# Preparing the first attention job one pair earlier, weight splits one by one, and loads in program order

## The chip, the cores and the metric

The kernel runs on one core of a Trainium2 chip. Its time is device microseconds, from runs on the chip: 737.43 us as a median of three runs (737.38 to 737.55). Every other time below is from one profiled execution of the kernel before, which took 735.49 us; its span, from the first recorded instruction to the last, is 733.8 us.

## The reference

Three stages follow each other; everything is float32.

```python
# attention: 2 batches, 8 heads, 576 rows, head size 64, causal, with a bias from cumulated s
scores = scale * q @ k.T;  cum = cumsum(max(s, 0))
scores = where(causal, -1e9, scores + min(-(cum_i - cum_j), 0))
x = softmax(scores) @ v                      # -> 1152 tokens x 512
# experts: all 4 for every token, weighted by p
out = sum over e of p[:, e] * (relu(x @ w1[e]) @ w2[e])      # 512 -> 1024 -> 512
# gated layer
y = ((out @ wa) * (out @ wb)) @ wo                           # 512 -> 1536 -> 512
```

## The kernel before

**How products are made.** Most products are made of three matmuls each: both operands are split into a high part that TensorE takes in its float32r format and a low part, the rest (`mm3`, line 276: high by high, high by low, low by high). A split is one copy on ACT (ScalarE) for the high part and one subtraction on VectorE (DVE) or GpSimd (POOL) for the low one. Weights are split this way too, in pieces of 512 KB: `load_next` (line 240) issues the load of a piece into one of three `raw` buffers, `split_next` (244) splits the oldest loaded one, `weight_step` (250) does one load and one split.

**The head.** Rows 0 to 255 of the first batch, for all eight heads, are done first, from `qk0` and `v0` (loop at line 896). Two heads make a pair; `pair_out` (line 832) divides the pair's result on VectorE (838), turns it on TensorE and copies it on ACT to `x32` (846) and to `xh` (847). There are four pairs.

**The attention.** What is left of the attention is cut into groups of row tiles, three of them, each with eight jobs, one per head. A job is loaded by `load_job` (569: `qr`, `kr`, and `kb` rows of the cumulated bias), prepared by `prep_job` (580: high part `qh` on ACT, low part `qb` on VectorE, high part `ks` on ACT, whose upper half goes by DMA into `kb` (589), and the low half of `ks` on GpSimd (590)), and then goes through one step per row tile: scores (616, 617), row maxima (627), exponential (639), division (644 to 646), transposes (657), their copies `eh` and `el` (672, 673), and the product with `v` (689). `attn_step` (919) issues one step; a step issues work of five tiles in different states, and at a job's first tile it prepares the job after it and loads the one after that. The scores need both halves of `ks` and, for the second matmul, `kb`.

**What runs beside it.** While the attention runs, TensorE does the first tokens' experts: a plain float32 expert (`mm1`, line 1023, on `x32` and `w32`), then expert 1 in split form. Behind the attention come the other experts and the gated layer, in units of their own with weight loads and splits at a pace of 3 us of a modelled clock.

**What sets the order.** The program is put in order by a scheduler that keeps each engine's own order as a list. Three things restrict it around the change. `tc.issue_after(i)` keeps the instructions of its block behind instruction `i` in that list; `gated` (234) does it for the instructions in `gate`, here the fourth pair's lines 838 and 846, and for the first three attention steps and the first two splits (`gated(n < 3)`, `gated(nsplits[0] < 3)`). `queued` (549) keeps loads in program order as long as `early[0]` is true, which ends with the third step or at the first call of `attn_step` that finds it false. And a modelled clock paces the weight steps: `run` (1272) calls `weight_step` once for every 4 us of it beside the attention.

Of the kernel before, what the change touches and what calls it, by code (L numbers as in the profile page):

```python
# [12 lines left out]
AF = mybir.ActivationFunctionType  # L13
# [46 lines left out]
def fused_kernel(ctx, tc, qk0, v0, qT, kT, v, s, dp, w1, w2, wa, wb, wo, out):  # L60
    nc = tc.nc
# [137 lines left out]
    def split_piece(r, key, form, wide, src, j):  # L199
        wh, wl = slabs[key]  # L200
        if form == "half" and wide:
            t = pools["cv"].tile([P, SL], I32, tag="t", name="t")
            narrow(t, r[:, :, 0], r[:, :, 1])
            split(wh[:, j, :], wl[:, j, :], t.bitcast(F32), nc.gpsimd)
        elif form == "half":
            split(wh, wl, r, nc.gpsimd)
        elif form == "pair" and wide:
            if j == 0:
                wides[key] = pools["cv"].tile([P, NC, 2 * P], I32, tag="tp", name="tp")
            t = wides[key]  # L210
            narrow(t[:, 2 * j : 2 * j + 2], r[:, :, :, 0], r[:, :, :, 1])
            if j:
                split_pair(key, t.bitcast(F32), nc.gpsimd)
        elif form == "pair":
            split_pair(key, r, nc.vector)
        else:
            nsplit[0] += 1
            lo_eng = nc.gpsimd if nsplit[0] % 2 or nsplit[0] <= NFIRST else nc.vector
            two = slice(2 * j, 2 * j + 2)
            if nsplit[0] <= NFIRST:  # L220
                nc.gpsimd.tensor_scalar(
                    out=wh[:, two, :], in0=r, scalar1=1.0, scalar2=1.0, op0=ALU.mult, op1=ALU.mult
                )
            else:
                nc.scalar.activation(out=wh[:, two, :], in_=r, func=AF.Copy)
            for m in (2 * j, 2 * j + 1):
                lo_eng.tensor_tensor(
                    out=wl[:, m, :], in0=r[:, m - 2 * j, :], in1=wh[:, m, :].bitcast(F32), op=ALU.subtract
                )

    gate = []
    nsplits = [0]

    def gated(on):
        x = ExitStack()
        for i in gate if on else ():
            x.enter_context(tc.issue_after(i))
        return x

# [4 lines left out]
    def split_next():  # L244
        r, p_ = loaded.pop(0)
        nsplits[0] += 1
        with gated(nsplits[0] < 3):
            split_piece(r, *p_)

    def weight_step():  # L250
# [296 lines left out]
    early = [False]  # L547

    def queued(ins):
        return in_order(ins) if early[0] else ins  # L550
# [6 lines left out]
    x32 = [ckr[:, o : o + NT0] for o in (3 * S, 0, NT0, 2 * NT0)]  # L557
# [11 lines left out]
    def load_job(j):  # L569
        b, h = j.b, j.h  # L570
        j.qh = io_p.tile([P, j.nq], F32R, tag="qh", name=f"qh{j.nm}")
        j.qb = qbs[(j.h + 1) % 2]
        j.qr = rw_p.tile([P, j.nq], F32, tag="qr", name=f"qr{j.nm}")
        j.kr = rw_p.tile([P, j.nk], F32, tag="kr", name=f"kr{j.nm}")
        j.kb = io_p.tile([RB, j.nk], F32R, tag="kb", name=f"kb{j.nm}")
        queued(nc.sync.dma_start(out=j.qr, in_=qT[b, h, :, j.q0 : j.q1]))
        queued(nc.sync.dma_start(out=j.kr, in_=kT[b, h, :, : j.nk]))
        queued(nc.sync.dma_start(out=j.kb[D:, :].bitcast(F32), in_=ckD[:, PLACE[j.gi], h, : j.nk]))
# [41 lines left out]
    def st_softmax(j, i):  # L620
        t = j.t[i]
        t.e = e_p.tile([P, t.n], F32, tag="e", name=f"e{j.nm}_{i}")
        m0 = S - t.n
        seed = 3.0e38
        for ps, c0, c1 in t.ps:
            mn = st_p.tile([P, 1], F32, tag="mn", name="mn")
            nc.vector.tensor_tensor_reduce(
                out=t.e[:, c0:c1],
                in0=ps,
                in1=causal[:, m0 + c0 : m0 + c1],  # L630
                scale=-1.0,
                scalar=seed,
                op0=ALU.add,
                op1=ALU.min,
                accum_out=mn,
            )
            seed = mn
        t.l = st_p.tile([P, 1], F32, tag="l", name="l")
        nc.scalar.activation(out=t.e, in_=t.e, func=AF.Exp, bias=mn, scale=-1.0, accum_out=t.l)

    def st_norm(j, i):
        t = j.t[i]
# [104 lines left out]
    for base in (0, -32, -64, -96):  # L747
        nc.gpsimd.affine_select(
            out=sel_, in_=sel_, pattern=[[-1, H]], compare_op=ALU.not_equal,
# [5 lines left out]
        out=causal[:, S - P :], in_=causal[:, S - P :], pattern=[[-1, P]], compare_op=ALU.is_ge, fill=MASKED,  # L755
# [6 lines left out]
        out=cum[:NS, :NT0], data0=ones[:NS, :NT0], data1=sc[:, :NT0], initial=0.0,  # L762
# [3 lines left out]
        out=cb, in0=cum[:NS, :NT0], scalar1=1.0, scalar2=1.0, op0=ALU.mult, op1=ALU.mult  # L766
    ))
    for lo_, eng in ((slice(32, NB), nc.vector), (slice(96, NS), nc.gpsimd)):
        in_order(eng.tensor_tensor(
            out=cb[lo_], in0=cum[lo_, :NT0], in1=cb[lo_].bitcast(F32), op=ALU.subtract  # L770
# [56 lines left out]
        if h % 2:  # L827
            keep_warm(1)

    last = {}  # L830

    def pair_out(j):
        av = heads["av"]
        l, r = (st_p.tile([P, 2, 2], F32, tag=t, name=t) for t in "lr")
        nc.vector.tensor_scalar(out=l, in0=av[:, :, :, D], scalar1=1e-9, scalar2=None, op0=ALU.add)
        nc.vector.reciprocal(out=r, in_=l)
        xq = x_p.tile([P, 2, 2, D], F32, tag=("xs", "xt")[j % 2], name="xq")
        last["dve"] = nc.vector.tensor_tensor(
            out=xq, in0=av[:, :, :, :D], in1=r.unsqueeze(3).broadcast_to([P, 2, 2, D]), op=ALU.mult
        )  # L840
        ps = ps_a.tile([P, NT0], F32, tag="av", name="xT")
        for t in range(2):
            nc.tensor.transpose(
                ps[:, t * P : t * P + P], xq[:, t].rearrange("p a d -> p (a d)"), ident
            )
        last["act"] = nc.scalar.activation(out=x32[j], in_=ps, func=AF.Copy)
        nc.scalar.activation(out=xh[j][:, :NT0], in_=ps, func=AF.Copy)
        nc.gpsimd.tensor_tensor(
            out=xl[j][:, :NT0], in0=x32[j], in1=xh[j][:, :NT0].bitcast(F32), op=ALU.subtract
        )  # L850
# [36 lines left out]
    def shares():  # L887
        nc.gpsimd.tensor_tensor(out=den, in0=pr[:, :, 0], in1=pr[:, :, 1], op=ALU.add)
        for e in range(2, E):
            nc.gpsimd.tensor_tensor(out=den, in0=den, in1=pr[:, :, e], op=ALU.add)  # L890
        nc.vector.tensor_scalar(out=den, in0=den, scalar1=1e-9, scalar2=None, op0=ALU.add)
        nc.vector.reciprocal(out=den, in_=den)
        for e in range(E):
            nc.gpsimd.tensor_tensor(out=pr[:, :, e], in0=pr[:, :, e], in1=den, op=ALU.mult)
# [21 lines left out]
    def at(n):  # L916
        return seq[n] if 0 <= n < len(seq) else None

    def attn_step():
        n = state["n"]  # L920
        early[0] = early[0] and n < 3
        with gated(n < 3):
            attn_work(n)

    def attn_work(n):
        state["n"] += 1
        passed.append([])

        if x := at(n):
            j, i = x  # L930
            if i == j.i0:
                k = jobs.index(j)
                if k + 1 < len(jobs):
                    prep_job(jobs[k + 1])
                if k + 2 < len(jobs):
                    load_job(jobs[k + 2])
            st_enter(j, i)
        if x := at(n - 3):
            st_transpose(*x)
        if x := at(n):  # L940
            st_scores(*x)
        if x := at(n - 2):
            st_norm(*x)
        if x := at(n - 1):
            st_softmax(*x)
        if x := at(n - 4):
            j, i = x
            if i == j.i1 - 1:
                st_av(j)
        if x := at(n - 3):  # L950
            st_evac(*x)
        if x := at(n):
            j, i = x
            if i == j.i0:
                prep_v(j)
                k = jobs.index(j)
                if k + 1 < len(jobs):
                    load_v(jobs[k + 1])
# [250 lines left out]
    queued(nc.sync.dma_start(out=pr, in_=dp))  # L1209
    for _ in range(3):  # L1210
        load_next()
    with tc.issue_after(last["act"].ins), tc.issue_after(last["dve"].ins):
        prep_job(jobs[0])
        load_job(jobs[1])
        shares()
    gate.extend((last["act"].ins, last["dve"].ins))

    def keys_of(k):
        return () if k is None else k if isinstance(k[0], tuple) else (k,)
# [2 lines left out]
    after = pipelined(  # L1222
        [plain_stage(w, m, *TURNS[-1]) for w in halves[1] for m in range(NPR)]
        + [relu_stage(ex, m) for ex, m in lasts]
        + [None]
        + [ab_stage(m) for m in range(NTH * NPR)],
        True,
    )

    n = [k for k, u in enumerate(after) if u[0] == ("w1", halves[1][1])][-1]  # L1230
# [12 lines left out]
    for n in range(len(seq) + 12):  # L1243
        x = at(n)
# [10 lines left out]
        lead.append((u0, turn_t[g + 1] - SLACK, ends[g], ends[g + 1]))  # L1255

    PACE, LATE_PACE = 4.0, 3.0
    clock = {"t": 0.0, "w": 0.0}

    def advance(us):  # L1260

# [91 lines left out]
```

## Time and profile before

| | |
|---|---|
| median of three runs | 737.43 us |
| profiled execution / its span | 735.49 / 733.8 us |
| TensorE busy | 714.9 us, 97% |
| VectorE, GpSimd, ACT busy | 70%, 55%, 44% of the span |
| DMA | 61.42 MB, mean 84 GB/s |

A matmul in the profile is busy from its start to its modelled end, so TensorE's 97% says when it had work, not that it worked at its peak. Idle time of an engine is put down to what ended it: `[1.53 <-POOL ks L590]` means that the engine stood idle for 1.53 us before this instruction and that line 590 on GpSimd released it. PEld is TensorE's loading of weights, SPq the queue of DMA issues on SyncE, PEclk the granted clock of TensorE as a share of 2.4 GHz.

### The profile page before, as it was taken

The numbers are of one execution on the slowest core, as the hardware profiler recorded it, in microseconds if no ns is written. First come the engines' busy times: TensorE is split into PE (matmuls) and PEld (weight loads), VectorE is DVE, ScalarE is ACT, GpSimd is POOL, SyncE is SP. The second block draws the span as 40 slices with busy tenths as digits, with TensorE's granted clock in tenths as the row PEclk, the third lists the DMA queues.
The fourth block names the chain that finished last, engine by engine and source line by source line (L and its number), as shares of the span: only waits on it lengthen the run. The fifth ranks groups of instructions, "written<-read, shape, count | busy, mean of one in ns | idle before, by whom it ended". The sixth has DMA issues, their size and how long they took to land.

```text
span 733.8 us, 10985 instructions
## 1 busy us (share of the span) xinstructions
PE 714.9 (97%) x3878; PEld 622.7 (85%) x3880; DVE 514.6 (70%) x1055; ACT 325.9 (44%) x722; POOL 402.6 (55%) x333
## 2 busy tenths in 40 slices
PE   9889999999999999999999999999899999999998
PEld 5777789999899888888888888887798888878886
DVE  5467788767595876665655566599773979798674
ACT  3578799877633332330323133334455424252410
POOL 5567666756225634431333057686478878888500
PEclk9989999999999999999999999999999999999999
DMA  8574333433021202211111021222022222222003
GB/s 325 170 224 134 80 94 110 135 101 99 10 87 57 87 30 64 74 54 39 57 58 32 26 87 58 87 86 87 30 79 65 87 87 81 92 73 72 1 0 130
DMA packets 33580, 61.42 MB, mean 84 GB/s; under 512 B 3269, under 2 KB 17253, under 8 KB 33525
## 3 DMA queue, kind: packets, MB, share of 16 engines
q1 hardware_dynamic: 33045, 59.61, 25.9%
q10 hardware_dynamic: 480, 1.11, 0.4%
q8 instruction: 31, 0.51, 0.3%
q14 instruction: 24, 0.20, 0.1%
HBM read 55.11 MB, written 2.58 MB: 79 GB/s over the span
## 4 chain that ended last, share of the span: by engine, by line
PE 77%; DVE 7%; POOL 5%; ACT 4%; issue 3%; DMA 3%; POOLq 0%; SPq 0%; ACTq 0%; DVEq 0%
PE ps L280 32%; PE psq L280 26%; PE pst L280 6%; PE av L689 3%; PE tr L657 2%; PE ps L1023 2%; POOL wl L81 2%; DMA kr<-in_kT 2%; POOL tp L162 1%; PE sc L617 1%; PE lullps L723 1%; PE sc L616 1%; PE av L823 1%; DVE tp L170 1%; DVE tp L174 1%
## 5 line engine op out<-in xcount | busy, mean ns | idle before, releaser
L280 PE MATMUL ps<-wh,h2h 128*128 128x512 f32 x332 | 130.7, 394 | 0.0
L280 PE MATMUL ps<-wl,h2h 128*128 128x512 f32 x332 | 129.6, 390 | 0.0
L81 POOL TENSOR_TENSOR wl<-raw,wh 128x1024 fp32r<-128x1024 f32 x24 | 58.2, 2432 | 129.0 <-ACT wh L80 98.6
L280 PE MATMUL ps<-wh,h2l 128*128 128x512 f32 x332 | 125.8, 392 | 0.0
L333 DVE SCALAR_TENSOR_TENSOR acc<-ps,pr,acc 128x512 f32<-128x512 f32 x111 | 82.3, 746 | 41.1 <-PE ps L280 40.4
L280 PE MATMUL psq<-xh,wh 128*128 128x448 f32 (+1 forms) x224 | 81.4, 363 | 0.0
L280 PE MATMUL psq<-xh,wl 128*128 128x448 f32 (+1 forms) x224 | 81.4, 363 | 0.0
L280 PE MATMUL psq<-xl,wh 128*128 128x448 f32 (+1 forms) x224 | 81.3, 363 | 0.0
L280 PEld LDWEIGHTS ps<-wh,h2l 128*128 128x128 f32 x332 | 62.2, 188 | 13.9 <-DVE h2l L81 0.7
L280 PEld LDWEIGHTS ps<-wh,h2h 128*128 128x128 f32 x332 | 62.4, 188 | 12.3 <-ACT h2h L80 0.7
L344 ACT ACTIVATE h2h<-psq 128x448 fp32r<-128x448 f32 (+1 forms) x56 | 29.5, 531 | 95.5 <-PE psq L280 76.2
L280 PEld LDWEIGHTS ps<-wl,h2h 128*128 128x128 f32 x332 | 62.4, 188 | 11.1
L81 POOL TENSOR_TENSOR wl<-sums,wh 128x1024 fp32r<-128x1024 f32 x24 | 58.2, 2425 | 6.0 <-ACT wh L80 6.0
L80 ACT ACTIVATE wh<-raw 128x1024 fp32r<-128x1024 f32 x24 | 25.5, 1062 | 69.4 <-PE ps L280 53.0
L280 PE MATMUL psq<-tqh,wh 128*128 128x448 f32 x144 | 53.0, 368 | 1.7 <-DVE h2l L81 1.5
L646 POOL TENSOR_SCALAR e<-e,r 128x448 f32<-128x448 f32 (+4 forms) x64 | 38.1, 600 | 26.8 <-DVE r L645 20.0
L280 PE MATMUL psq<-tql,wh 128*128 128x448 f32 x144 | 52.6, 365 | 0.0
L280 PE MATMUL psq<-tqh,wl 128*128 128x448 f32 x144 | 52.5, 364 | 0.0
L673 DVE TENSOR_TENSOR el<-tr,eh 128x512 fp32r<-128x512 f32 (+5 forms) x80 | 38.4, 484 | 18.2 <-ACT eh L672 17.4
L162 POOL TENSOR_SCALAR tp<-tp 128x512 f32<-128x512 f32 x24 | 47.2, 1981 | 5.9 <-ACT tp L161 5.9
L431 DVE TENSOR_TENSOR u<-psq,s 128x448 f32<-128x448 f32 x48 | 29.7, 619 | 27.3 <-PE psq L280 24.8
L280 PE MATMUL pst<-xh,wh 128*128 128x256 f32 x160 | 44.9, 281 | 2.8 <-DVE xl L81 2.7
(199 smaller groups left out, 1897.9 us busy)
## 6 DMA issues: line engine op xcount, KB each, us to landing
raw<-in_w SPq DMA_DIRECT2D x32, 512.0 KB
raw<-in_wa SPq DMA_DIRECT2D x12, 512.0 KB
raw<-in_wb SPq DMA_DIRECT2D x12, 512.0 KB
raw<-in_wo SPq DMA_DIRECT2D x12, 512.0 KB
kr<-in_kT SPq DMA_DIRECT2D x16, 288.0 KB
w<-in_w SPq DMA_DIRECT2D x8, 512.0 KB
vr<-in_v SPq DMA_DIRECT2D x16, 160.0 KB
kb<-ks SPq DMA_DIRECT2D x16, 144.0 KB
```

The lines of the kernel that those rows point to most:

```text
L80: nc.scalar.activation(out=hi, in_=src, func=AF.Copy)
L81: lo_eng.tensor_tensor(out=lo, in0=src, in1=hi.bitcast(F32), op=ALU.subtract)
L162: nc.gpsimd.tensor_scalar(out=t.bitcast(F32), in0=t.bitcast(F32), scalar1=2.0**-15, scalar2=GMAX, op0=ALU.max, op1=ALU.min,)
L280: ins = nc.tensor.matmul(ps, lhsT=l, rhs=r, start=first and k == 0, stop=last and k == 2, skip_group_check=more)
L333: nc.vector.scalar_tensor_tensor(out=dst, in0=ps, scalar=share, in1=dst, op0=ALU.mult, op1=ALU.add)
L344: nc.scalar.activation(out=hh, in_=src, func=AF.Relu)
L431: nc.vector.tensor_tensor(out=out, in0=a, in1=b, op=ALU.add)
L646: nc.gpsimd.tensor_scalar(out=t.e, in0=t.e, scalar1=r, scalar2=1.0, op0=ALU.mult, op1=ALU.mult)
L657: ins = nc.tensor.transpose(ps[:, c - c0, :], t.e[:, k0 : k0 + P], ident)
L673: nc.vector.tensor_tensor(out=j.el[:, c0:c1, x], in0=src, in1=hi.bitcast(F32), op=ALU.subtract)
L689: ins = nc.tensor.matmul(ps[:, o:], lhsT=j.vs[:, c, :], rhs=e[:, c, o:], start=(m == 0), stop=(m == len(mms) - 1),)
L1023: ins = nc.tensor.matmul(ps, lhsT=w, rhs=x, start=start, stop=stop)
```

## The change

Job 0's preparation, and the load of job 1, are kept behind the third pair's instructions, not the fourth's; the shares of the experts (`shares`) and the first three attention steps are kept behind both. Each of the first eight weight splits is kept behind the last exponential that was issued before it. Loads stay in program order for the first eight attention steps. The modelled clock of the weight steps starts at 6 us.

```diff
-    def gated(on):
+    exps = []
+    def gated(after):
         x = ExitStack()
-        for i in gate if on else ():
+        for i in after:
             x.enter_context(tc.issue_after(i))
         return x
...
     def split_next():
         r, p_ = loaded.pop(0)
         nsplits[0] += 1
-        with gated(nsplits[0] < 3):
+        with gated(exps[-1:] if nsplits[0] < 9 else ()):
             split_piece(r, *p_)
...
-        nc.scalar.activation(out=t.e, in_=t.e, func=AF.Exp, bias=mn, scale=-1.0, accum_out=t.l)
+        exps.append(
+            nc.scalar.activation(out=t.e, in_=t.e, func=AF.Exp, bias=mn, scale=-1.0, accum_out=t.l).ins
+        )
...
-    last = {}
+    last = []
...
-        last["dve"] = nc.vector.tensor_tensor(
+        x = nc.vector.tensor_tensor(
...
-        last["act"] = nc.scalar.activation(out=x32[j], in_=ps, func=AF.Copy)
+        y = nc.scalar.activation(out=x32[j], in_=ps, func=AF.Copy)
+        last.append((x.ins, y.ins))
...
     def attn_step():
         n = state["n"]
-        early[0] = early[0] and n < 3
-        with gated(n < 3):
+        early[0] = n < 8
+        with gated(gate if n < 3 else ()):
             attn_work(n)
...
-    with tc.issue_after(last["act"].ins), tc.issue_after(last["dve"].ins):
+    gate.extend(last[-2])
+    with gated(gate):
         prep_job(jobs[0])
         load_job(jobs[1])
+    gate.extend(last[-1])
+    with gated(gate):
         shares()
-    gate.extend((last["act"].ins, last["dve"].ins))
...
-    clock = {"t": 0.0, "w": 0.0}
+    clock = {"t": 0.0, "w": 6.0}
```

In the rows below, `ks_1_2_468` is `ks` of job 1 (head 1 of the group whose first tile is 2), and the last figure is a buffer's number. Lines of the changed kernel are up to four higher.

ACT, from the third pair's copies on, before:

```order
L846 ACTIVATE ckr<-xT 128x256
L847 ACTIVATE xh<-xT 128x256
L846 ACTIVATE ckr<-xT 128x256
L847 ACTIVATE xh<-xT 128x256
L583 ACTIVATE qh_0_2_422<-qr_0_2_423 128x384
L588 ACTIVATE ks_0_2_442<-kr_0_2_424 128x576
L80 ACTIVATE vs_0_2_484<-vr_0_2_429 128x5x64
L225 ACTIVATE wh<-raw 128x1024 x2
L1042 ACTIVATE h_490<-ps_464 128x256
L583 ACTIVATE qh_1_2_448<-qr_1_2_449 128x384
```

and ACT at the same place now:

```order
L849 ACTIVATE ckr<-xT 128x256
L851 ACTIVATE xh<-xT 128x256
L584 ACTIVATE qh_0_2_422<-qr_0_2_423 128x384
L589 ACTIVATE ks_0_2_442<-kr_0_2_424 128x576
L849 ACTIVATE ckr<-xT 128x256
L851 ACTIVATE xh<-xT 128x256
L80 ACTIVATE vs_0_2_484<-vr_0_2_429 128x5x64
L584 ACTIVATE qh_1_2_448<-qr_1_2_449 128x384
L589 ACTIVATE ks_1_2_468<-kr_1_2_450 128x576
```

Job 0's two copies moved in front of the fourth pair's, and the two weight splits (`wh<-raw`) that stood ahead of job 1's `qh` are gone from here.

SyncE, the loads from job 2's `kr` on, before:

```order
L577 DMA kr_2_2_476<-in_kT 128x576
L578 DMA kb_2_2_477<-ckD 3x576
L596 DMA vr_1_2_487<-in_v 128x320
L156 DMA raw<-in_w 128x1024 x2
L576 DMA qr_3_2_539<-in_qT 128x384
L589 DMA kb_2_2_477<-ks_2_2_532 64x576
L156 DMA raw<-in_w 128x1024
L578 DMA kb_3_2_541<-ckD 3x576
L577 DMA kr_3_2_540<-in_kT 128x576
```

and SyncE at the same place now:

```order
L578 DMA kr_2_2_476<-in_kT 128x576
L579 DMA kb_2_2_477<-ckD 3x576
L597 DMA vr_1_2_487<-in_v 128x320
L590 DMA kb_2_2_477<-ks_2_2_527 64x576
L577 DMA qr_3_2_534<-in_qT 128x384
L578 DMA kr_3_2_535<-in_kT 128x576
L579 DMA kb_3_2_536<-ckD 3x576
L597 DMA vr_2_2_565<-in_v 128x320
L156 DMA raw<-in_w 128x1024
L590 DMA kb_3_2_536<-ks_3_2_635 64x576
```

The two weight pieces that stood ahead of job 2's `kb<-ks` are gone from there; one now stands ahead of job 3's.

## Rows read from the trace of the kernel before

**Rows 1.** The page: span, and busy time of TensorE.

```profile
span 733.8 us, 10985 instructions
PE 714.9 (97%) x3878; PEld 622.7 (85%) x3880; DVE 514.6 (70%) x1055; ACT 325.9 (44%) x722; POOL 402.6 (55%) x333
```

**Rows 2.** Stretches: length, busy PE, PEld, DVE, ACT, POOL (instructions), PEclk, DMA share, GB/s.

```profile
30.00:40.00 10.00, 8.15 (x32) 6.38 (x31) 7.10 (x16) 7.65 (x17) 8.23 (x8) 0.83 0.35 86
40.00:50.00 10.00, 7.22 (x41) 6.03 (x39) 6.20 (x20) 6.90 (x20) 7.44 (x8) 1.00 0.97 281
50.00:60.00 10.00, 9.88 (x54) 8.94 (x55) 6.42 (x20) 8.71 (x22) 6.23 (x6) 0.83 0.50 154
...
100.00:120.00 20.00, 19.33 (x151) 18.29 (x151) 15.32 (x62) 18.80 (x72) 13.03 (x21) 1.00 0.38 104
34.40:37.70 3.30, 3.30 (x10) 2.55 (x9) 3.30 (x5) 2.14 (x7) 3.10 (x3) 0.50 0.16 55
51.50:54.80 3.30, 3.30 (x14) 3.12 (x14) 1.45 (x6) 2.98 (x9) 1.98 (x2) 0.50 0.55 169
```

**Rows 3.** TensorE's waits: us in total, times, longest.

```profile
PE pst L280 <- DVE xl L81: 2.7, 1, 2.7
PE sc L617 <- DMA kr<-in_kT: 2.1, 1, 2.1
PE sc L616 <- POOL ks L590: 1.5, 1, 1.5
...
PE psq L280 <- DVE h2l L81: 1.5, 1, 1.5
...
PE sc L616 <- DVE el L673: 0.8, 1, 0.8
PE sc L616 <- DVE mn L627: 0.6, 1, 0.6
```

**Rows 4.** Timeline, 25 to 34 us: start, us, instruction, [idle before <-releaser].

```profile
25.65 0.38 ACT L846 ACTIVATE ckr<-xT 128x256 f32<-128x256 f32 x1 [1.16 <-PE xT L843]
...
26.39 0.72 POOL L848 TENSOR_TENSOR xl<-ckr,xh 128x256 fp32r<-128x256 f32 x1 [0.22 <-ACT xh L847]
...
29.84 0.52 ACT L583 ACTIVATE qh<-qr 128x384 fp32r<-128x384 f32 x1
...
30.25 0.68 ACT L588 ACTIVATE ks<-kr 128x576 fp32r<-128x576 f32 x1
...
31.06 1.40 POOL L590 TENSOR_TENSOR ks<-kr,ks 64x576 fp32r<-64x576 f32 x1 [0.30 <-ACT ks L588]
...
32.52 0.61 PE L616 MATMUL sc<-ks,qh 128*128 128x320 f32 x2 [1.53 <-POOL ks L590]
...
33.45 0.59 PE L617 MATMUL sc<-kb,qb 67*128 67x320 f32 x2 [0.32 <-issue]
```

**Rows 5.** Timeline, SyncE's issues of `kb` and of weight pieces.

```profile
30.96 0.56 SPq L589 DMA_DIRECT2D kb<-ks  x1
...
40.59 0.90 SPq L156 DMA_DIRECT2D raw<-in_w  x2
...
42.95 0.47 SPq L589 DMA_DIRECT2D kb<-ks  x1
43.47 0.60 SPq L156 DMA_DIRECT2D raw<-in_w  x1
```

**Rows 6.** Timeline, job 2: its keys' copy on ACT, its second matmul.

```profile
42.25 0.67 ACT L588 ACTIVATE ks<-kr 128x576 fp32r<-128x576 f32 x1
...
50.12 0.58 PE L617 MATMUL sc<-kb,qb 67*128 67x320 f32 x2 [2.07 <-DMA kr<-in_kT]
```

**Rows 7.** Groups by line, 28 to 50 us: count | busy us, mean ns | idle before.

```profile
L227 POOL TENSOR_TENSOR wl<-raw,wh 128x512 fp32r<-128x512 f32 x4 | 5.8, 1478 | 0.0
...
L225 ACT ACTIVATE wh<-raw 128x1024 fp32r<-128x1024 f32 x4 | 4.1, 1054 | 1.7 <-DMA raw<-in_w 1.2 <-PE ps L1023 0.4
```

**Rows 8.** SyncE's waits, 15 to 110 us, at the weight load.

```profile
SPq L156 <- DVE wl L227: 1.4, 1, 1.4
```

## The prediction

> **What bounds the kernel now.** I read the page's head first: a span of 733.8 us in which TensorE is busy for 714.9 us, 97% [rows 1]. Nothing else is near that, so time is only to be had where TensorE waits or runs at half rate. The table by stretches, which has the granted clock, shows two holes: the mean granted clock is 0.83 in 30 to 40 us and again in 50 to 60 us, and inside them 34.4 to 37.7 us and 51.5 to 54.8 us stand at 0.50, the lower of the two levels, with TensorE busy for all 3.30 us of each [rows 2]. A mean of 0.83 over 10 us is 0.17 x 10 = 1.7 us of work at full rate that is missing in each. The view of TensorE's waits then names what ended them [rows 3]: the largest in the early part are 2.1 us for a load of the attention, 1.5 us for the low half of keys (`ks`, line 590) and 0.8 us for a VectorE copy; later there are one of 2.7 us at the turn of the accumulators and one of 1.5 us in the last stage. In 30 to 50 us TensorE is busy 8.15 + 7.22 of 20 us, in 100 to 120 us 19.33 of 20 [rows 2]: the early attention steps are the only place where several microseconds lie together, and that is where the change works.
>
> The two holes of the clock each follow a wait. TensorE waits 1.53 + 0.32 us up to 33.45 us [rows 4] and is at half rate from 34.4 us; it waits 0.83 us and then 2.07 us up to 50.12 us [rows 3, 6] and is at half rate from 51.5 us. The Trainium skill says in "TensorE: Matmul & The Clock Gate", section "What's actually happening", that the throttled state is the default and that activity releases it. By that rule the holes go with the waits, and the trace agrees as far as it goes, with two holes behind two waits; left out, the sum would be 3.4 us smaller.
>
> **The change, part by part.** First, job 0 of group 1 (queries, keys and their low parts) is prepared behind the third pair of the head, not the fourth. Now ACT copies `qh` at 29.84 and `ks` at 30.25 us, right behind the fourth pair's copies; GpSimd makes the low half of `ks` from 31.06 for 1.40 us, and TensorE, which has nothing else in its order before the scores, gets them at 32.52 us [rows 4]. In the new order ACT has both copies between the third and the fourth pair. The third pair's copy to `x32` starts at 25.65 us and GpSimd's third `xl` at 26.39, ending at 27.11 us [rows 4]; with `qh` from about 26.3 and `ks` from about 26.7, 0.68 us long, GpSimd can begin at 27.4 and end at 28.8 us. TensorE asks for it now at 32.52 - 1.53 = 30.99 us; the new order has two matmuls of the plain expert fewer in front, so it asks at about 30 us, and there is 1.2 us of cover; if `ks` were later than that, the wait is back microsecond for microsecond. The other operand, the low part `kb`, goes by DMA from `ks` and took 30.96 to 33.45 us, 2.5 us [rows 4, 5]; issued at 27.4 us it is there at 29.9. What is moved also puts `qb`, one VectorE instruction, ahead of the fourth pair's; TensorE has matmuls of the plain expert to run meanwhile. Bounds: nothing of 1.85 us saved, or all of it. I take all but 0.3 us: **1.55 us**. Behind it the half-rate stretch, between nothing and 1.7 us; I take **1.7 us**.
>
> Second, the splits. Of the eight early weight pieces, four are split between 28 and 50 us: ACT 4.1 us in four copies of 1054 ns, GpSimd 5.8 us in four halves of 1478 ns [rows 7], the other halves on VectorE. Now two run at once on ACT, ahead of job 1's `qh`. The new order has none before job 1's first exponential. The work isn't gone: four splits leave this stretch and come one by one between later steps, as eight then do, up to job 6. There ACT has less room: in 100 to 120 us it is already busy 18.80 of 20 us, and TensorE loses only 0.67 us [rows 2]. So of 4 x 1.054 = 4.2 us of ACT time that is pushed there, TensorE feels between less than nothing (the 0.6 us behind the row maxima, line 627 [rows 3], could go, since the splits no longer stand in front of them in pairs) and all 4.2 us. The nearest row, the one at 100 to 120 us, says that a stretch with ACT at 94% costs some 3%; over the 40 us between 45 and 85 us that is 1.3 us. I charge **1.5 us**.
>
> Third, the loads. At 40.59 and 43.47 us three weight pieces of 512 KB are issued ahead of or around job 2's `kb`, which is issued at 42.95 us [rows 5]; its matmul starts at 50.12 us [rows 6], 7.2 us later, against 2.5 us for job 0, whose `kb` has the queue to itself. In 40 to 50 us the DMA engines are busy 0.97 of the time at 281 GB/s [rows 2]: 1.5 MB at that rate is 5.6 us, which is the delay. (The view writes the wait down to `kr`; the instruction that waits reads `kb`.) In the new order no weight piece stands between the first three and job 2's `kb`; the fourth piece comes behind job 3's `qr`, `kr`, `vr`. So the 2.07 us go, and the 0.83 us before, where VectorE's `el` had a split in front of it, should. Bounds: zero and 2.9 us; I leave 0.4 us for a transpose buffer that ACT frees late, since its order there is `e`, split, `h`, `eh`: **2.5 us**. And the second half-rate stretch, between nothing and 1.7 us: **1.7 us**.
>
> Fourth, the clock of the weight steps starts at 6 and not 0. Up to the end of the attention only these eight pieces can be loaded, so the shift shows in the late stages alone, as a step that falls one unit earlier or later. The order of TensorE is the same from the attention's end to a place behind the turn, so the wait of 2.7 us [rows 3] stays; behind it the matmuls of tails and quadrants swap places. There is one wait of 1.5 us in that part now [rows 3]. It may go, or a second one like it may come: plus or minus 1.5 us; I take 0, since the pieces, durations and engines there are the same and TensorE is never short of them by more than that one row.
>
> **Sum.** 1.55 + 1.7 + 2.5 + 1.7 - 1.5 = 5.95 us. The profiled execution took 735.49 us, 1.7 us more than its span, and would take 729.5; the runs shown have a median of 737.43, 1.9 us above the profiled one, so the forecast is 737.43 - 5.95, rounded **731.4 us**. With all terms at their good ends: 1.85 + 1.7 + 2.9 + 1.7 + 0.6 + 1.5 = 10.3 us, 727.1.
>
> **Rivals.** *Only the first hole closes.* TensorE reaches job 2 earlier, but its `ks` hangs on a chain (load of `kr` after job 1's `ks` is free, ACT, DMA) that gets no shorter: it takes over the wait of about 2 us, and the clock falls once more. Then 1.55 + 1.7 - 1.5 = 1.75 us, **735.7 us**. For it: the order keeps job 2's `kr` behind job 1's `ks` on GpSimd. Against it: job 1's `ks` moves forward too, with no split in front of it, by the same 3 to 4 us.
>
> *Nothing comes of it.* The first steps are paced by ACT and GpSimd (busy 7.65 and 8.23 of 10 us in 30 to 40 us [rows 2]), and what TensorE no longer waits for in one place it waits for in the next: **737.4 us**. Against it: with four splits out of 30 to 50 us ACT falls from 14.55 to 10.4 us of 20 there.
>
> *Slower: the weight loads hold up the queue.* The first steps' loads now stand on SyncE in program order. A fourth piece waits there until the first piece's split on GpSimd has freed its buffer, and job 3's `kb` stands behind it; the fifth and later pieces stand so in front of jobs 4, 5 and 7. SyncE has such a wait now too, 1.4 us behind a VectorE split [rows 8]. The Trainium skill speaks for this one: "DMA: Bandwidth & Descriptors", section "Anatomy of one DMA — SWDGE (gpsimd) path", says that DMA engines do not wait on semaphores and that a wait is served by the issuing sequencer before dispatch. The row of 1.4 us agrees. Job 3 has some cover: job 2's keys are copied at 42.25 us and TensorE asks for `kb` at 50.12 - 2.07 = 48.05, 5.8 us later [rows 6]; if job 3 has the same, 2.5 us of it are the DMA and 1.9 us (512 KB at 281 GB/s) the piece ahead, so this decides from 1.4 us of delay on. If three of the four jobs came late by what job 2 does now, 2.07 us with a half-rate stretch of 1.7 us each, that is 11.3 us against a gain of 7.45: **741.3 us**.
>
> **Chances.** Forecast 0.68, with a range of its own of 728.5 to 733.5; only the first hole 0.17; nothing 0.06; slower 0.09. The range of 728.0 to 736.5 us takes in the forecast's case with most of the late term, and the first rival to its slow side; outside it lie most of the last two and the edges. About 0.2%, 1.5 us, is what runs of this kernel can tell from no change, that is 736.0 to 738.9 us. Faster: 0.67 of the forecast's case and 0.11 of the first rival, 0.78. Same: the rest of that rival and the second, 0.12. Slower: 0.10.
>
> **What will show it.** In the table by stretches the granted clock is 1.00 in both 30 to 40 and 50 to 60 us; if either reads 0.83, that step is wrong. In TensorE's waits the rows for `ks` (1.5 us) and for `kr` (2.1 us) are gone, and no new row among the attention's is over 1 us; GpSimd's low half of `ks` for job 0 begins near 27.4 us; job 2's `kb` lands some 2.5 us after its issue. The rival of the queue would show as SyncE waits at the weight load of 2 us and more, with TensorE waits for `kb` at jobs 3 to 7. The charge of 1.5 us would show as more waits in 45 to 90 us than now. The prediction as a whole is wrong if the scores of job 2 start less than 4 us earlier than 50.1 us, or if what is won there is lost again before 130 us.

## The result: 729.9 us, some 1% faster

The changed kernel took 729.93 us (median of four runs, 728.68 to 730.32), beside 737.49 us for the kernel before (737.38 to 738.12) on the same chip: ratio 0.990, 95% interval 0.9876 to 0.9924. The forecast was 731.4 us, and its range holds the time. The profiled execution took 729.56 us against 735.49.

The page of the profile after, its span and TensorE's busy time (before: [rows 1]):

```profile
span 727.8 us, 10965 instructions
PE 712.1 (98%) x3880; PEld 621.7 (85%) x3880; DVE 511.8 (70%) x1055; ACT 324.8 (45%) x722; POOL 400.5 (55%) x333
```

The span fell by 6.0 us. TensorE's idle time, span less busy, fell from 18.9 to 15.7 us, and its busy time by 2.8 us, of which 1.7 is one half-rate stretch fewer. The same stretches as in [rows 2], and one behind the turn (columns as there):

```profile
30.00:40.00 10.00, 9.94 (x52) 8.70 (x51) 5.40 (x20) 7.35 (x22) 5.93 (x7) 1.00 0.47 128
40.00:50.00 10.00, 9.24 (x59) 8.12 (x57) 8.14 (x25) 9.17 (x28) 8.39 (x10) 1.00 0.66 179
50.00:60.00 10.00, 9.39 (x50) 6.90 (x51) 8.10 (x25) 8.37 (x22) 8.49 (x10) 1.00 0.65 186
100.00:120.00 20.00, 18.83 (x132) 17.16 (x131) 16.21 (x64) 18.47 (x72) 12.30 (x22) 1.00 0.37 102
510.90:514.20 3.30, 3.30 (x14) 3.08 (x13) 3.30 (x5) 1.12 (x2) 1.33 (x2) 0.50 0.00 0
```

In 30 to 50 us TensorE is busy 19.18 of 20 us instead of 15.37, and the granted clock is 1.00 from 30 to 60 us. But 510.9 to 514.2 us is now at half rate. That is behind the wait at the turn, the place where the experts' finished sums are transposed and split for the gated layer. TensorE's waits after (us in total, times, longest; [rows 3]):

```profile
PE pst L281 <- DVE xl L81: 2.7, 1, 2.7
PE tr L660 <- DVE el L676: 1.5, 4, 0.6
...
PE tr L660 <- DVE r L648: 1.3, 2, 0.7
PE av L692 <- DVE el L676: 1.2, 3, 0.8
PE sc L617 <- DVE mn L628: 1.0, 1, 1.0
PE psq L281 <- DVE h2l L81: 0.9, 3, 0.4
```

The rows for `ks` (1.5 us) and `kr` (2.1 us) are gone; smaller waits for VectorE came in their place. One that grew passes the 1 us that the prediction named as a limit: `av` behind `el`, 1.2 us in three waits. The timeline of jobs 0 and 2 ([rows 4 to 6]; the second part starts at SyncE's issue of job 2's `kb`):

```profile
26.31 0.68 ACT L589 ACTIVATE ks<-kr 128x576 fp32r<-128x576 f32 x1
...
27.02 0.56 SPq L590 DMA_DIRECT2D kb<-ks  x1
...
27.12 1.40 POOL L591 TENSOR_TENSOR ks<-kr,ks 64x576 fp32r<-64x576 f32 x1 [0.30 <-POOL xl L852]
...
29.47 0.70 PE L617 MATMUL sc<-ks,qh 128*128 128x320 f32 x2
...
37.72 0.47 SPq L590 DMA_DIRECT2D kb<-ks  x1
...
43.69 0.31 PE L618 MATMUL sc<-kb,qb 67*128 67x320 f32 x1
```

Job 0's low half of `ks` ends at 28.5 us and its scores start at 29.47 without a wait; job 2's second matmul starts at 43.69 us instead of 50.12. SyncE's waits at the weight load, 15 to 110 us ([rows 8]):

```profile
SPq L156 <- POOL wl L227: 3.7, 2, 2.1
SPq L156 <- DVE wl L227: 1.0, 1, 1.0
```

The queue does stand still at the weight load, up to 2.1 us, as the slower rival had it, but no wait for `kb` follows on TensorE. The timeline shows why for job 3:

```profile
43.10 0.69 ACT L589 ACTIVATE ks<-kr 128x576 fp32r<-128x576 f32 x1 [0.46 <-issue]
...
43.43 0.33 SPq L156 DMA_DIRECT2D raw<-in_w  x1
43.85 0.47 SPq L590 DMA_DIRECT2D kb<-ks  x1
```

The weight piece goes out before the copy of the keys ends at 43.79 us, and `kb` follows that copy by 0.06 us. The other piece that waited goes out at 55.57 us, and the next `kb`, that of job 5, leaves at 59.68, again right behind its copy on ACT. In neither of these two places did the piece hold up `kb`.

### The profile page after: what moved, and what is told of

Same layout as the page of the kernel before. It is cut to its first block, busy times and chain, and to the rows that moved or that the text cites. A ratio compares the mean times of both kernels' runs of the same rounds, so it can differ in the third digit from the quotient of the medians.

```text
span 727.8 us, 10965 instructions
## 1 busy us (share of the span) xinstructions
PE 712.1 (98%) x3880; PEld 621.7 (85%) x3880; DVE 511.8 (70%) x1055; ACT 324.8 (45%) x722; POOL 400.5 (55%) x333
## 4 chain that ended last, share of the span: by engine, by line
PE 66%; DVE 13%; POOL 8%; issue 5%; ACT 4%; DMA 3%; SPq 0%; POOLq 0%; ACTq 0%; DVEq 0%
PE ps L281 29%; PE psq L281 22%; PE pst L281 5%; POOL wl L81 3%; PE av L692 2%; PE tr L660 2%; PE ps L1027 2%; POOL tp L162 1%; DVE tp L174 1%; DVE tp L170 1%; DVE h2l L81 1%; DMA kr<-in_kT 1%; DVE acc L1202 1%; ACT e L641 1%; DVE tp L166 1%
```

## Experiments: the parts apart

Ratios are to runs of the kernel before on the same chip, whose medians were 736.2 to 736.9 us.

**Part 1 alone** (`prep_only`): only job 0's preparation is moved.

```diff
+    gate.extend(last[-2])
+    with gated(gate):
         prep_job(jobs[0])
         load_job(jobs[1])
+    gate.extend(last[-1])
+    with gated(gate):
         shares()
```

> The kernel before with the first part alone: job 0 prepared behind the head's third pair; splits, loads and clock start as before. If the prediction's first two terms are right, the waits of 1.53 and 0.32 us before job 0's scores and the half-rate stretch of 34.4 to 37.7 us go, and the time is 3.25 us below the kernel before (about 734.2 us). Rival, what is won there is waited for again at job 2, whose loads still stand behind three weight pieces: then the wait at job 2 grows from 2.07 us towards 4 us, the half-rate stretch behind it stays, and the time is within 1 us of before.

Measured: 738.14 us, ratio 1.0032 (1.0015 to 1.0049): slower than before. Timeline, SyncE and TensorE, from job 1's `kb`:

```profile
32.90 0.49 SPq L589 DMA_DIRECT2D kb<-ks  x1
...
38.08 0.89 SPq L156 DMA_DIRECT2D raw<-in_w  x2
...
41.33 0.47 SPq L589 DMA_DIRECT2D kb<-ks  x1
...
48.12 0.59 PE L617 MATMUL sc<-kb,qb 67*128 67x320 f32 x2 [2.19 <-DMA kr<-in_kT]
...
60.59 0.41 PE L616 MATMUL sc<-ks,qh 128*128 128x320 f32 x1 [3.23 <-DVE mn L627]
```

VectorE and GpSimd ahead of that last wait, and then VectorE at the same step in the kernel before, where TensorE waits 0.63 us:

```profile
55.51 2.94 DVE L227 TENSOR_TENSOR wl<-raw,wh 128x512 fp32r<-128x512 f32 x2
58.37 1.75 DVE L584 SCALAR_TENSOR_TENSOR qb<-qr,qh 64x384 fp32r<-64x384 f32 x1
60.05 0.47 DVE L627 CUSTOM_DVE_ANT_0 e<-sc,causal 128x320 f32<-128x320 f32 x1
...
54.93 2.97 POOL L227 TENSOR_TENSOR wl<-raw,wh 128x512 fp32r<-128x512 f32 x2
57.98 1.74 POOL L590 TENSOR_TENSOR ks<-kr,ks 64x576 fp32r<-64x576 f32 x1
...
58.20 1.55 DVE L227 TENSOR_TENSOR wl<-raw,wh 128x512 fp32r<-128x512 f32 x2
59.67 0.90 DVE L584 SCALAR_TENSOR_TENSOR qb<-qr,qh 64x384 fp32r<-64x384 f32 x1
```

The lead of 4 us at job 0 is down to 1.6 at job 2's `kb`, behind two weight pieces, and a split and `qb`, which stand on VectorE ahead of the row maxima, take the rest. They stand there in the kernel before too, but take 4.69 us here and 2.45 there. Here GpSimd is at its own halves and at `ks` for nearly all of that time, there mostly at a division; in the changed kernel `qb` takes 0.55 us at 35.97 us, with GpSimd idle, and 1.76 at 50.77, beside `ks`. So the two engines' work has slid together; no run tests this by itself. The half-rate stretch at 34 us is gone, as expected, but one now stands behind the wait of 3.23 us and one at the turn. What is won at job 0 is lost again, as the rival had it, but not where it said: job 2's wait is 2.19 us, hardly more than before (2.07), the larger wait comes behind it, and the kernel is 1.6 us slower than before, not within 1 us of it.

**All but part 1** (`after_noprep`): the changed kernel with `gate.extend(last[-1])` ahead of `prep_job(jobs[0])`.

> The changed kernel with job 0 prepared behind the head's fourth pair as before; all else as changed. By the prediction's first two terms 3.25 us slower than the changed kernel, about 733.2 us, with the wait of about 1.85 us before job 0's scores and a mean granted clock of 0.83 in 30 to 40 us. If only the wait counts and the half-rate stretch is not tied to it, 1.55 us slower and a clock of 1.00. If what is lost there is won back at the next waits, within 0.5 us of the changed kernel.

Measured: 737.22 us, ratio 1.0016 (0.9998 to 1.0035). All of the gain is gone, more than twice the 3.25 us of the first two terms. The wait at job 0 is back as it was, and two more come behind it. Timeline, TensorE:

```profile
32.20 0.61 PE L617 MATMUL sc<-ks,qh 128*128 128x320 f32 x2 [1.53 <-POOL ks L591]
...
45.13 0.42 PE L692 MATMUL av<-eh,vs 128*128 128x320 f32 x1 [1.61 <-ACT eh L675]
...
54.16 0.63 PE L660 MATMUL tr<-ident,e 128*128 128x128 f32 x4 [1.52 <-DVE el L676]
```

The clock stays at 1.00 behind job 0's wait here (33.5 to 40 us), so the expectation's tie between the two failed too. Against the changed kernel's profile, this one has 4.7 us more of idle time and one half-rate stretch more.

**Loads in order for three steps alone** (`after_n3`).

```diff
-        early[0] = n < 8
+        early[0] = early[0] and n < 3
```

> The changed kernel with loads kept in program order for the first three steps alone, as before. If the program order of the loads is what brings job 2's keys in time (third step of the prediction), the wait at job 2 of about 2 us and the half-rate stretch of 1.7 us come back: 4 us slower than the changed kernel, about 734 us. Rival, the splits tied one by one to the exponentials and the weight steps that start 6 us later already keep the weight pieces behind job 2's keys: then the time is that of the changed kernel, 730 us within 1 us. Only two pairs of small loads on SyncE and one weight piece change places here, which speaks for the rival.

Measured: 729.95 us, ratio 0.9918 (0.9894 to 0.9942): the changed kernel's time. With the other edits in place, program order beyond the third step changes nothing that can be measured; the rival's time held.

**Clock start undone** (`after_w0`), and **undone with the first split held** (`after_w0_gated`).

```diff
-    clock = {"t": 0.0, "w": 6.0}
+    clock = {"t": 0.0, "w": 0.0}
...
-        with gated(exps[-1:] if nsplits[0] < 9 else ()):
+        with gated((exps[-1:] or gate) if nsplits[0] < 9 else ()):   # after_w0_gated only
```

> The changed kernel with the clock of the weight steps starting at 0 as before. The prediction put this edit at nothing (within 1.5 us) and in the late stages alone: then 730 us. Rival: the later start is what keeps weight pieces out of SyncE's queue ahead of job 2's and job 3's keys; with it undone one more piece of 512 KB stands ahead of each, and the kernel loses from 1.9 us (one piece at 281 GB/s) to 4 us with a half-rate stretch: 732 to 734 us.

Measured: 736.66 us, ratio 1.0014 (0.9987 to 1.0041). Timeline, ACT and TensorE in the head:

```profile
25.34 1.06 ACT L225 ACTIVATE wh<-raw 128x1024 fp32r<-128x1024 f32 x1 [4.65 <-DMA raw<-in_w]
...
26.74 0.84 PE L813 MATMUL tr<-ident,e 128*128 128x128 f32 x3 [2.42 <-ACT e L805]
```

With the clock at 0 the first weight step comes before any attention step, so there is no exponential to hold its split. It stands on ACT between the copies of the head's first and second pair (20.04 and 27.36 us; the next expectation says third and fourth) and waits for its weights, and the head's transposes wait for ACT. Job 0's scores start at 34.4 us. The profile has four half-rate stretches, one of them behind this wait, where the changed kernel's has one: of the 8.1 us between the two spans, 5.1 are the three stretches more and 2.9 idle time. The rival said that weight pieces ahead of the keys would cost 2 to 4 us; the loss is larger, 6.7 us, and begins elsewhere, so the second kernel holds that split behind the fourth pair:

> The changed kernel with the clock of the weight steps at 0, and the first split, which then has no exponential to be tied to, held behind the head's last pair. With the clock at 0 alone the first split stood on ACT between the head's third and fourth pair, waited 4.65 us for its weights, and TensorE waited 2.42 us. If that is the whole of what the later start is worth, this kernel is within 0.7 us of the changed one. If the later start also pays by keeping weight pieces out of the queue ahead of the keys of jobs 2 and 3, this one still loses 1 to 3 us, with a wait for `kb` at job 2 or 3.

Measured: 731.91 us, ratio 0.9937 (0.9913 to 0.9961). Most of the loss was that one split; some 2 us are left, and job 2's `kb` goes out at 39.52 us instead of 37.72, behind one weight piece at 36.70. No wait for `kb` showed; the waits that grew are for VectorE's `el` and GpSimd's division (1.1 and 1.2 us), and one of 1.3 us for VectorE near the turn, so not all of the 2 us is shown to come from the queue.

**Splits as before** (`after_oldsplits`).

```diff
-        with gated(exps[-1:] if nsplits[0] < 9 else ()):
+        with gated(gate if nsplits[0] < 3 else ()):
```

> The changed kernel with the first two splits held behind the head's last pair and the other six free, as before, in place of one by one behind the exponentials. Theory: the splits tied to the exponentials keep ACT free for the keys of jobs 1 and 2; undone, two splits of 1.05 us stand on ACT ahead of job 1's queries, as before, and waits come back at jobs 1 and 2: 2 to 4 us slower without the half-rate stretches (each of which has cost 1.7 us in every profile so far). Rival: the later start of the weight steps alone keeps the splits away from these keys, and tying them does nothing: within 0.5 us of the changed kernel. The prediction charged the moved splits with 1.5 us; by that alone this kernel would be 1.5 us faster.

Measured: 734.89 us, ratio 0.9981 (0.9962 to 1.0000), 5 us above the changed kernel. Timeline, ACT and SyncE, then one of TensorE's waits:

```profile
29.81 2.00 ACT L225 ACTIVATE wh<-raw 128x1024 fp32r<-128x1024 f32 x2
31.70 0.52 ACT L584 ACTIVATE qh<-qr 128x384 fp32r<-128x384 f32 x1
...
41.08 0.47 SPq L590 DMA_DIRECT2D kb<-ks  x1
...
53.09 0.63 PE L660 MATMUL tr<-ident,e 128*128 128x128 f32 x4 [1.89 <-DVE el L676]
```

Two splits stand ahead of job 1's `qh` again, and job 2's `kb` goes out 3.4 us later than in the changed kernel. The profile has one half-rate stretch more than the changed kernel's (53 to 58 us), so the 5 us fit the theory's 2 to 4 without stretches. The theory held; the charge of 1.5 us had the wrong sign.

**The chain cut.** SyncE's issues of `kb<-ks`, from the timelines, in us:

| kernel | job 0 | job 1 | job 2 | job 3 | job 4 | time |
|---|---|---|---|---|---|---|
| before | 30.96 | 36.42 | 42.95 | 52.48 | 59.18 | 737.5 |
| changed | 27.02 | 32.16 | 37.72 | 43.85 | 50.58 | 729.9 |
| `prep_only` | 27.01 | 32.90 | 41.33 | 50.51 | 56.43 | 738.1 |
| `after_noprep` | 30.65 | 36.54 | 43.59 | 49.79 | 55.40 | 737.2 |
| `after_oldsplits` | 26.93 | 32.82 | 41.08 | 48.28 | 54.29 | 734.9 |

Of these, only the changed kernel keeps its lead over the kernel before at every job, 3.9 us at job 0 and 8.6 at jobs 3 and 4. The lead is a sign and not a price: at job 4 `after_noprep` is 3.8 us ahead of the kernel before and takes as long, and `prep_only` is 2.8 us ahead and slower. A job's loads go into the buffers that the copies of the job before free, so the jobs form a chain with 5 to 7 us a link in the changed kernel. ACT keeps its order, so where it reaches a job's copies before their loads have landed it stands still with the copies `eh` and the exponentials queued behind. ACT's waits for these loads, 33 to 56 us, in `after_noprep`:

```profile
ACT qh L584 <- DMA qr<-in_qT: 4.6, 3, 2.7
ACT ks L589 <- DMA kr<-in_kT: 1.8, 2, 1.3
```

and all that the changed kernel has of them:

```profile
ACT qh L584 <- DMA qr<-in_qT: 1.5, 2, 1.4
```

That is 6.4 us against 1.5 (the kernel before: 3.1). Two buffers, and loads issued one job ahead, cut the chain:

```diff
+    rw2_p = actx.enter_context(tc.tile_pool(name="rw2", bufs=2))     # for qr and kr
...
                 if k + 2 < len(jobs):
                     load_job(jobs[k + 2])
+                if k + 1 < len(jobs):
+                    prep_job(jobs[k + 1])
```

(with `load_job(jobs[1])` right behind `load_job(jobs[0])`, and 10 hidden buffers for 11.)

> The changed kernel with two buffers in place of one for the queries and keys as loaded (and one buffer fewer for hidden tiles, 10 for 11, to make room), and each job's loads issued ahead of the preparation of the job before it. New theory: the early attention steps hang on one chain, in which job k+1's loads wait until job k's copies have freed the only buffer, about 5 to 7 us for a link (keys copied at 26.3, 31.5, 37.0, 43.1 and 49.9 us in the changed kernel); a lead at its start is kept only if no link is held up. With two buffers the chain is cut: 0 to 1.5 us faster than the changed kernel, since few of its waits are left (4.1 us in 40 to 132 us). Rival: the waits that are left hang on the softmax and the transposes alone: same time within 0.5 us.

Measured: 730.77 us, ratio 0.9926 (0.9912 to 0.9940): no faster than the changed kernel. ACT waits for none of these loads in 33 to 56 us, but it had little of that left to lose. The rival's time held, but its reason isn't shown, for the edit also moves a wait to SyncE. Its waits for a free `kb` buffer in 28 to 53 us (the changed kernel: 3.5 us) and job 1's `kb`, whose keys were copied by 30.55 us:

```profile
SPq L580 <- PE sc L619: 11.5, 3, 4.5
...
34.62 0.26 SPq L580 DMA_DIRECT2D kb<-ckD  x1
34.97 0.49 SPq L591 DMA_DIRECT2D kb<-ks  x1
```

The next job's `kb` rows now stand in SyncE's order ahead of this job's `kb<-ks`. The `kb` of jobs 1 to 3 goes out at 34.97, 42.16 and 51.47 us, 3 to 8 us later than in the changed kernel, and job 0's low half of `ks` starts at 29.44 us instead of 27.12, for which TensorE waits 1.15 us. That the time is the same even so says once more that the time doesn't follow the issue of `kb` alone.

> The same two buffers, with job 0 prepared behind the head's fourth pair as before. With one buffer this cost 7 us against the changed kernel (737.2 against 730), of which only 1.9 us was the wait at job 0. If the rest was the chain (jobs 1 to 4 prepared 4 to 6 us later), it costs 2 to 3.5 us here, for job 0's wait and a half-rate stretch at most. Rival: TensorE's steps are late because job 0's scores are late, whatever the loads do: then 5 to 7 us again.

Measured: 733.36 us, ratio 0.9961 (0.9945 to 0.9976). The late job 0 costs 2.6 us here and 7.3 with one buffer, and ACT's 6.4 us of waiting are gone. So the larger part of what `after_noprep` lost came by way of the loads. (Buffers and order of the loads were changed together, and with them SyncE's order, as above; which of them does it wasn't parted. That ACT's waits are the link is the reading that fits, not one that was tested alone.)

> The kernel before with the same two buffers and early loads, none of the change. If the chain of loads is what the change loosens, this recovers a part of its gain: job 2's wait of 2.07 us for its keys goes, 2 to 4 us below before. If the splits on ACT ahead of the keys are the link that holds, nothing: ACT's copies of the keys still stand behind two splits, and the time is within 1 us of before.

Measured: 735.08 us, ratio 0.9979 (0.9959 to 0.9998). Job 2's wait of 2.07 us is gone, and 1.8 us of the change's 7 are had this way, just short of the expected 2 to 4; job 0's wait is still there (1.8 us), one of 2.0 us for `el` is new, and the profile has three half-rate stretches.

**The clock** (`before_warm`): idle matmuls into the scores' bank ahead of jobs 0 and 2.

```diff
+            for _ in range({0: 12, 2: 14}.get(jobs.index(j), 0) if c0 == 0 and i == j.i0 else 0):
+                nc.tensor.matmul(ps, lhsT=j.qh[:, q0 : q0 + P], rhs=j.qh[:, : c1 - c0], start=True, stop=True)
```

> The kernel before with idle matmuls on TensorE in its two early waits: 12 of 320 columns ahead of job 0's scores and 14 ahead of job 2's, into the bank that the scores then overwrite. The waits are no shorter in time, but TensorE is busy in them. If each half-rate stretch follows from the wait ahead of it (as the prediction's terms of 1.7 us had it), the stretches at 34 and 51 us go, and the time is 3.4 us below before, less at most 0.5 us for idle matmuls that outlast the waits. Rival, the stretches come by chance at one of many waits: they turn up behind another wait, and the time is within 1 us of before.

Measured: 739.48 us, ratio 1.0044 (1.0025 to 1.0062): slower. Stretches and TensorE's largest waits:

```profile
30.00:40.00 10.00, 8.70 (x46) 7.28 (x45) 7.17 (x16) 7.73 (x17) 8.38 (x8) 1.00 0.34 85
...
50.00:60.00 10.00, 8.84 (x55) 7.58 (x55) 6.91 (x19) 8.93 (x24) 7.24 (x8) 1.00 0.50 151
518.00:523.00 5.00, 5.00 (x27) 4.77 (x27) 5.00 (x8) 1.60 (x4) 2.19 (x2) 0.66 0.01 3
```

```profile
PE sc L618 <- DVE mn L629: 4.8, 3, 2.8
```

The two half-rate stretches are not there, and one stands at the turn instead, where the kernel before had none in its profile. But the idle matmuls also changed TensorE's order from 52 us on, and waits for row maxima grew to 4.8 us. The longest, 2.83 us, is at the step of `prep_only`'s 3.23 us, again with a slow split and `qb` on VectorE ahead of it (2.65 and 1.75 us). What the two stretches are worth by themselves stays open.

**Two tries at a faster version.** `after_w12` starts the clock at 12.0; `after_turn` finishes tiles 7 and 8 behind tiles 0 to 3 and turns them first:

```diff
-            tiles = [*range(0,7*P,P),7*P,8*P]
+            tiles = [t * P for t in (0, 1, 2, 3, 7, 8, 4, 5, 6)]
...
+            l2 = l2[:4] + LOW + l2[4:6] + REST + l2[6:] + HIGH + [SUMS_]
```

> The changed kernel with the clock of the weight steps at 12 in place of 6: no weight piece stands in SyncE's queue ahead of job 3's or job 4's keys, and the first splits come later still. By the prediction's first and third steps the start does nothing: 730 us. If each weight piece and split that leaves the first jobs' chain is worth 0.5 to 1 us, as between 0 (731.9 us with the first split held back) and 6 (730 us), 1 to 2 us faster than the changed kernel: 728 to 729 us. If the pieces are then late for their own stage, or crowd the later jobs, slower.

> The changed kernel with another order at the turn of the accumulators: tiles 7 and 8 are finished behind tiles 0 to 3, and their transposes and splits (line 1160) come ahead of those of the higher half. The wait of 2.73 us at the turn was TensorE's matmuls of the last two tiles behind VectorE's splits of them, which stood behind nine VectorE steps of the higher half. If nothing else becomes late, the wait goes and the half-rate stretch behind it with it where there was one: 2.7 us faster than the changed kernel, 4.4 at most. Rival: the sums of the higher half, which now come last, are late instead, and the wait moves to their matmuls: within 1 us of the changed kernel.

Measured: 730.08 us, ratio 0.9914 (0.9900 to 0.9928), and 730.95 us, ratio 0.9926 (0.9898 to 0.9953). Neither beats the changed kernel. In `after_w12`, beyond the three pieces of the start, no weight piece goes out ahead of the `kb` of any of jobs 0 to 4, so the pieces ahead of jobs 3 and 4 cost the changed kernel nothing that shows. In `after_turn` the 2.7 us at the turn became this:

```profile
513.75 0.47 PE L281 MATMUL psq<-xh,wh 128*128 128x448 f32 x1 [1.41 <-ACT sr L1182]
```

and half a dozen waits of 0.4 to 0.7 us behind it.

## Why the prediction came out right, step by step

**The whole.** 5.95 us were forecast, 5.93 are between the two profiled executions, 7.56 between the medians; before's profiled one lay 2.0 us under its median and after's 0.4 under its own. (737.43 - 5.95 is 731.48, which the prediction rounds to 731.4.) The sum of the waits was too low (1.55 + 2.5 - 1.5 = 2.55, measured 3.2 of idle time) and that of the clock too high (3.4, measured 1.7), with 1.1 us of busy time that no step names. It fits because these errors cancel, and that is luck, the clock above all. TensorE's first matmul behind the wait at the turn, before and after:

```profile
516.68 0.39 PE L280 MATMUL pst<-xh,wh 128*128 128x256 f32 x1 [2.74 <-DVE xl L81]
...
509.64 0.39 PE L281 MATMUL pst<-xh,wh 128*128 128x256 f32 x1 [2.73 <-DVE xl L81]
```

Up to there the changed kernel leads by 7.0 us, with both stretches gone; the stretch behind it takes 1.7 back, and the kernel before, with the same wait, had none there. Nor is the gain mainly the clock's: at a mean granted clock of 0.998 three executions of the changed kernel took 728.7 to 730.3 us, and sixteen of the kernel before, on the experiments' chips, 734.1 to 737.5.

**First step, job 0.** As forecast: GpSimd began at 27.12 us (forecast 27.4), the waits of 1.53 and 0.32 us are gone, and there is 0.95 us of cover (forecast 1.2). But it is no term that can be added: alone it gains nothing, and without it the rest gains nothing. The rival in which the gain is waited for again is what happens when only this part is made, though the wait that grows stands behind job 2's.

**Second step, splits.** The step failed. It took them as work moved to a fuller place, at 1.5 us. TensorE is idle for somewhat longer behind 50 us, as it said (3.5 us instead of 2.9 in 50 to 130 us), but the edit is what keeps the lead of job 0: undone, it costs 5 us. Nor did ACT empty in 30 to 50 us: it was to fall from 14.55 to 10.4 us and is busy 16.52, since the steps themselves come earlier.

**Third step, loads.** Half right. No weight piece stands ahead of job 2's `kb`, and its wait is gone, but not by the edit that keeps the loads in program order: `after_n3` shows no difference. The later clock start keeps the pieces away: with the splits untied (`after_oldsplits`) the first goes out at 45.51 us, behind job 2's `kb` at 41.08, and with the clock at 0 (`after_w0_gated`) one stands ahead of it.

**Fourth step, clock start.** The step failed: "the shift shows in the late stages alone". It decides where the first split stands; undone it costs 6.7 us, 2 of them still with that split held. I had read what the start of 6 delays, and not that a split with no exponential ahead of it is held by nothing.

**Half-rate stretches.** Both went from their places, as forecast, and one came at the turn. The same wait comes with such a stretch and without: see below.

**The queue's rival** had SyncE's wait, 2.1 us at the weight load, but not what stands behind it: in both places the piece was out before the keys were copied, so `kb` wasn't late by it.

## What to carry to other kernels

Where small loads share one set of buffers, read the jobs as one chain, compare the time of each link between kernels and look at how long the copying engine waits for loads in its own order. A lead can be lost at any link, so the parts of such a change can't be priced one by one from the waits that they remove, and undoing each part tells more than making each alone. When work is tied behind "the last instruction of a kind", look at what holds it before the first one exists.

## What was not expected of the hardware

The half-rate stretches cost 1.7 us each, and the profiled execution had two before and one after. The same wait of 2.7 us at the turn had one at its end in ten of the thirteen profiles that show the wait, not in the one of before, of `after_w0_gated` and of `noprep_rw2`; job 0's wait, where it was 1.5 us or more, by one in three of four profiles. The Trainium skill ("TensorE: Matmul & The Clock Gate", section "What's actually happening") calls the cold stretch at a kernel's start run-variable; these runs show the same in mid-kernel. Part of the spread goes with it: nine executions of the kernel before with a mean granted clock of 1.000 took 733.6 to 734.7 us, sixteen at 0.995 took 735.2 to 736.7; but those at 0.998 lie between 734.1 and 737.5, so the clock is not all of it. A difference of 2 us between two profiles of this kernel is no evidence until the stretches in both are counted.
